# Late-mode forms in 128 rows, and fillers that move TensorE's instruction fetches, in a fused linear-attention and spectral-mix kernel

## The chip, the cores and the metric

The kernel runs on one core of a Trainium2 chip. The time is the device time of that core in microseconds (us), as the median of several executions. Before the change it was 421.37 us over 3 runs (421.35 to 421.74). The profile is one further execution of the same program; its span, from the first instruction to the last, was 419.6 us before. A stretch of the trace is given in us from the start of that span.

Besides the views of the profile, this document uses the packet records of the trace: start, duration, queue and size of every DMA packet. They carry no engine number; the *packets in flight* are counted over all engines together. A load of weights or a store ends with 16 small completion marks, one from each DMA engine, and the distance from the first mark to the last is called its *spread* here.

## The reference, cut to what matters

```python
def _attn_ref(q, k, v):                       # (8, 8, 576, 64) each
    q_p, k_p = (phi(q), phi(k))
    kv = np.einsum('bhsd,bhse->bhde', k_p, v)
    ...
    return (num / den).astype(np.float32)

def _moe_ref(x, w_r, w_i, w_ch):              # w_r, w_i: (64, 512, 512), w_ch: (512, 512)
    X = np.fft.rfft(x, axis=1)
    Xr, Xi = (np.real(X[:, :n_modes]), np.imag(X[:, :n_modes]))
    Yr = np.einsum('bmd,mde->bme', Xr, w_r) - np.einsum('bmd,mde->bme', Xi, w_i)
    Yi = np.einsum('bmd,mde->bme', Xr, w_i) + np.einsum('bmd,mde->bme', Xi, w_r)
    Y[:, :n_modes] = Yr + 1j * Yi
    y = np.fft.irfft(Y, n=S, axis=1)
    u = x + y
    return (u + np.maximum(u @ w_ch, 0.0)).astype(np.float32)
```

The 64 modes have two 512x512 weight matrices each. These are the bulk of the bytes, and each is used only once.

## The kernel before: the parts concerned

The modes are worked off in pairs. For each pair the weights arrive in one of two rotating buffers, TensorE makes the product `P`, and the result is turned into columns (`picks`). After every fourth pair eight modes are evicted from PSUM. Modes from 32 on ("late") go to `YL`. Work of the attention part and of the end is put between, in slots, and *fillers* (`keep_warm`, products of the identity whose result nobody reads) end a pair.

```python
    def keep_warm(n: int):
        for _ in range(n):
            pin(nc.tensor.matmul(last_ps[0], id16, wch16[:, 0, :]))
    ...
    def mode_pair(p: int):
        w = w_get(p)
        ...
        for dc in range(NDW):
            product(P, xz[p % 2][:, dc].rearrange("p h n -> p (h n)"), 32, w, dc, NDW)
        ...
        work_slot(p, "mid")
        picks(2 * p, st, 2)
        if p % 4 == 3:
            ...
                g = (kk - NF) // NL + 1
                pin(nc.vector.tensor_copy(out=YL[:, :, :, g, :], in_=mode_rows(yt_ps)))
        work_slot(p, "end")
        keep_warm(FILL.get(p, 0))
    ...
    FILL = {**{p: 7 for p in range(18, 27)}, 27: 9, 28: 5, 29: 6, 30: 4}
```

In the last pairs each batch's late modes are brought into two forms, `z` (times `w_ch`) and `y` (transposed). `YL` holds the rows of a batch once, 64 of them, and both halves of the 128 output rows are made from them by a matmul each:

```python
    def form_z(b: int):
        z_ps = bank(f"z{b}")
        for ec in range(NDC):
            yt = YL[:, ec].rearrange("p k g b -> p (k g) b")[:, :, b]
            for h in range(2):
                pin(nc.tensor.matmul(z_ps[HALVES[h], :], yt, wch16[:, ec, :], ...))
        pin(nc.scalar.copy(out=YZ[b][:, 1, :], in_=z_ps))
```

## Time and profile before

| quantity | before | view |
|---|---|---|
| time, median of 3 | 421.37 us | timed runs |
| end of the weights' stage | 387.71 us | chain of work that ended last |
| last rows' copy issued, after which stores run | 390.30 us | timeline |
| last store's marks | 417.52 to 418.09 us | packet records |
| instruction fetches of TensorE, the last of them | 24, at 396.4 us | queue table, packet records |

First the page: one line of the engines' busy time, and two groups of instructions (busy us and mean ns of one; after the second bar the idle time before them and what ended it).

```profile
PE 288.7 (69%) x3115; PEld 155.9 (37%) x3115; DVE 228.6 (54%) x499; ACT 154.2 (37%) x253; POOL 58.1 (14%) x100
...
L431 PE MATMUL P<-w,xz 128*32 128x512 bf16 x496 | 48.3, 530 | 64.3 <-DMA w<-in_moe_w_i_dram 61.8
...
L418 PE MATMUL zl<-wch,id 128*128 128x512 f16 x93 | 23.0, 380 | 0.0
```

The products of the pairs (L431) wait 64.3 us in sum, 61.8 of it for weights: TensorE is not what bounds this stage. The fillers (L418) wait for nothing. The forms and the late eviction, in the view of the tile `YL` (ns: least, median, largest; then first and last start):

```profile
L710 PE MATMUL z<-wch,YL x64: 379/379/493, 352.6 to 380.3; 128*64 128x512 f16 x64
...
L480 DVE CAST YL<-yt x3: 681/691/692, 276.1 to 351.8; 128x512 f16<-128x512 f32 x3
```

There are 64 half-wide `z` matmuls and three large evictions. Last, a row of the table of windows from the stretch without fillers (columns: length, busy us of PE, PEld, DVE, ACT and POOL with counts, clock, DMA share, GB/s):

```profile
157.00:176.00 19.00, 7.20 (x88) 2.96 (x87) 6.00 (x18) 1.89 (x5) 1.77 (x5) 0.50 1.00 214
```

TensorE is busy 7.20 of 19 us, at half clock, with DMA full.

### The profile page before, as it was taken

How to read it: one execution, taken by the hardware profiler on the slowest of the kernel's cores; microseconds unless marked ns; L12 is line 12 of the kernel's file. 1: busy time of each engine (PE TensorE's matmuls, PEld its weight loads, DVE VectorE, ACT ScalarE, POOL GpSimd, SP SyncE). 2: the span in 40 equal slices, each digit the busy share in tenths (PEclk: the TensorE clock that was granted, in tenths of full speed). 3: DMA queues.
4: the chain of work that ended last, by engine and by line, in shares of the span. 5: the costliest groups of instructions: out<-in, count | busy, mean ns of one | idle time of the engine just before them, and what ended most of it. 6: DMA issues, size and time to landing. Idle time of an engine off the chain costs nothing.

```text
span 419.6 us, 7400 instructions
## 1 busy us (share of the span) xinstructions
PE 288.7 (69%) x3115; PEld 155.9 (37%) x3115; DVE 228.6 (54%) x499; ACT 154.2 (37%) x253; POOL 58.1 (14%) x100
## 2 busy tenths in 40 slices
PE   0359799899517553444343685998798878899993
PEld 0247677787301221222121232433343324354421
DVE  4587979994404462464645353454455433512794
ACT  4677888954101011000000233344253422230782
POOL 4222224210001111111111111111111111130000
PEclk9999958989655555555555589799899989999997
DMA  8999999999999999999999999999999999998698
GB/s 219 211 212 216 210 221 206 229 206 222 222 217 212 213 223 211 216 222 209 220 220 205 225 220 205 225 215 209 224 217 208 225 216 209 223 205 162 230 395 328
DMA packets 17073, 93.17 MB, mean 222 GB/s; under 512 B 2112, under 2 KB 3024, under 8 KB 12880
## 3 DMA queue, kind: packets, MB, share of 16 engines
q0 software_dynamic: 12496, 81.48, 93.3%
q1 hardware_dynamic: 4544, 11.22, 7.2%
q8 instruction: 24, 0.39, 0.3%
q14 instruction: 9, 0.07, 0.0%
HBM read 163.93 MB, written 9.44 MB: 413 GB/s over the span
## 4 chain that ended last, share of the span: by engine, by line
DMA 65%; PE 19%; DVE 5%; issue 3%; ACT 3%; POOL 2%; DVEq 0%; ACTq 0%; POOLq 0%
DMA w<-in_moe_w_i_dram 52%; DMA pick_sb<-row_pick 8%; PE P L431 7%; DMA k<-in_k_dram 5%; PE acc L747 3%; PE acc L787 2%; PE kvp L256 2%; ACT ke L207 2%; POOL w L116 2%; PE eps L688 1%; DVE x L292 1%; DVE ke L220 1%; POOL w L128 1%; DVE k L214 1%; PE zl L418 0%
## 5 line engine op out<-in xcount | busy, mean ns | idle before, releaser
L431 PE MATMUL P<-w,xz 128*32 128x512 bf16 x496 | 48.3, 530 | 64.3 <-DMA w<-in_moe_w_i_dram 61.8
L448 ACT CAST ys<-P 128x512 f16<-128x512 f32 x15 | 8.8, 585 | 131.6 <-PE P L431 131.6
L116 POOL DMA_DIRECT2D w<-in_moe_w_r_dram x31 | 17.8, 575 | 244.2 <-PE P L431 240.7
L431 PEld LDWEIGHTS <-xz 128*32 128x32 bf16 x496 | 13.2, 115 | 85.5 <-DMA w<-in_moe_w_i_dram 56.9
L446 DVE CAST ys<-P 128x512 f16<-128x512 f32 x17 | 11.8, 691 | 53.5 <-PE P L431 53.5
L688 PE MATMUL eps<-wch,xTw 128*128 128x512 f16 x144 | 40.6, 409 | 0.0
L162 PEld LDWEIGHTS <-qT 64*128 64x128 f16 (+1 forms) x640 | 22.8, 124 | 31.7 <-issue 17.2
L671 ACT CAST x16w<-x_main 128x512 f16<-128x512 f32 x32 | 19.8, 618 | 37.7 <-DVE x_main L669 37.7
L669 DVE TENSOR_TENSOR x_main<-ya,x_main 128x512 f32<-128x512 f32 x32 | 22.0, 691 | 18.7 <-PE ya L665 18.5
L256 PE MATMUL kvp<-vpad,ke 32*128 32x130 f16 x576 | 23.3, 255 | 9.1 <-ACT qT L243 6.4
L441 DVE COPY xz<-xt_c 64x256 bf16<-64x256 bf16 x62 | 22.9, 370 | 12.1 <-PE P L431 11.3
L696 ACT CAST E<-eps 128x512 f16<-128x512 f32 (+1 forms) x40 | 21.2, 539 | 19.5 <-PE eps L688 19.5
L256 PEld LDWEIGHTS <-ke 32*128 32x128 f16 x576 | 21.4, 113 | 10.8 <-issue 8.9
L162 PE MATMUL nw<-kv,qT 64*128 64x65 f16 (+1 forms) x320 | 18.9, 240 | 9.5 <-DVE x_tail L632 4.5
L418 PE MATMUL zl<-wch,id 128*128 128x512 f16 x93 | 23.0, 380 | 0.0
L292 DVE TENSOR_TENSOR x<-num,rd 128x512 f16<-128x512 f32 x32 | 22.1, 692 | 1.1
L236 PE MATMUL qTp<-id,qe 128*128 128x128 f16 x144 | 14.3, 278 | 11.7 <-DVE qe L220 9.5
L632 DVE TENSOR_TENSOR x_main<-nw,rd 128x256 f32<-128x256 f32 x32 | 11.2, 417 | 17.3 <-PE nw L162 17.3
L207 ACT ACTIVATE qe<-q 128x1152 f16<-128x1152 f16 (+1 forms) x16 | 17.9, 1157 | 7.5 <-DMA q<-in_q_dram 7.4
L454 PE MATMUL yt<-pick_sb,ys 128*128 128x32 f16 (+1 forms) x128 | 8.8, 186 | 16.9 <-DMA pick_sb<-row_pick 10.7
L680 DVE COPY xTw<-xTp 128x512 f16<-128x512 f16 x36 | 15.0, 416 | 10.0 <-PE xTp L678 9.9
L243 ACT COPY qT<-qTp 128x1152 f16<-128x1152 f16 x16 | 19.6, 1291 | 0.5 <-PE qTp L236 0.2
(118 smaller groups left out, 494.6 us busy)
## 6 DMA issues: line engine op xcount, KB each, us to landing
w<-in_moe_w_r_dram POOLq DMA_DIRECT2D x31, 1024.0 KB, 12.5
w<-in_moe_w_i_dram POOLq DMA_DIRECT2D x31, 1024.0 KB, 16.7
out_dram<-x_main SPq DMA_DIRECT2D x12, 512.0 KB, 3.8
k<-in_k_dram POOLq DMA_DIRECT2D x8, 576.0 KB, 13.1
v<-in_v_dram POOLq DMA_DIRECT2D x8, 576.0 KB, 14.4
q<-in_q_dram POOLq DMA_DIRECT2D x7, 576.0 KB, 12.8
out_dram<-x_main SPq DMA_DIRECT2D x8, 256.0 KB, 3.8
q<-in_q_dram SPq DMA_DIRECT2D x2, 576.0 KB, 4.5
```

The source lines that it names most:

```text
L116: nc.gpsimd.dma_start(out=w_in[p][half::2], in_=two.rearrange("g (r dc) e -> (g r) dc e", dc=NDW))
L162: mm = nc.tensor.matmul(num[hpo][orow, c0 : c0 + 65], qT[rows, hpp, h2, cols], kv_sb[rows, hpp, h2, :])
L207: pin(nc.scalar.activation(out=ev[:, c], in_=heads(nm, b, c), func=AF.Exp))
L256: nc.tensor.matmul(kv_ps[:, h2, 0:130], phi["k", b][r0 : r0 + 32, j // NJ, j % NJ].rearrange("p o d -> p (o d)"), vp[r0 : r0 + 32, :, j, 0 ...
L292: nc.vector.tensor_tensor(out=dst.rearrange("p (o c d) -> p o c d", o=2, c=4), in0=nv[:, :, :, 0:64], in1=rden.unsqueeze(3).broadcast_to([ ...
L418: pin(nc.tensor.matmul(last_ps[0], id16, wch16[:, 0, :]))
L431: nc.tensor.matmul(P[c : c + n, :], x, w[:, dc, :], start=(dc < NDC), stop=(dc >= n_dc - NDC), tile_position=(0, c), skip_group_check=True,)
L441: pin(nc.vector.tensor_copy(out=xz[p % 2][HALVES[h], :, h, :], in_=src))
L669: pin(nc.vector.tensor_tensor(out=x, in0=acc, in1=x, op=ALU.add))
L671: pin(nc.scalar.copy(out=x16w[t], in_=x))
L688: nc.tensor.matmul(e_ps, xT[:, c, :], wch16[:, c, :], start=(c == 0), stop=(c == NDC - 1))
L696: pin(nc.scalar.copy(out=dst, in_=e_ps[:, cols]))
```

## The change

The rows of a batch are kept twice in `YL`, now split over two tiles, so that one full-width matmul makes all 128 rows of a form: 64 matmuls fewer. The forms move out of pair 30, and pairs 28 to 30 get more fillers in their place. Pairs 5 to 15 (modes 10 to 31) get seven fillers each. By the words of the change these are there to shift TensorE's instruction fetches.

```diff
-    FILL = {**{p: 7 for p in range(18, 27)}, 27: 9, 28: 5, 29: 6, 30: 4}
+    FILL = {**{p: 7 for p in range(5, 16)}, **{p: 7 for p in range(18, 27)}, 27: 7, 28: 10, 29: 12, 30: 10}
...
+    def late_modes(g: int, ps):
+        ...
+        for h, yl in enumerate(YL):
+            rows = mode_rows(ps)[:, h * (NDC // 2) : h * (NDC // 2) + NDC // 2]
+            for d in range(2):
+                pin(nc.vector.tensor_copy(out=yl[:, :, d, :, g, :], in_=rows))
...
         for ec in range(NDC):
-            yt = YL[:, ec].rearrange("p k g b -> p (k g) b")[:, :, b]
-            for h in range(2):
-                pin(
-                    nc.tensor.matmul(
-                        z_ps[HALVES[h], :], yt, wch16[:, ec, :],
-                        start=(ec == 0), stop=(ec == NDC - 1), skip_group_check=True,
-                    )
-                )
+            pin(
+                nc.tensor.matmul(
+                    z_ps, late_rows(ec, b), wch16[:, ec, :], start=(ec == 0), stop=(ec == NDC - 1)
+                )
+            )
...   (form_y in the same way)
     share(
         n_form,
-        [((first_form, "end"), 6)]
+        [((first_form, "end"), 8)]
         + [((p, h), 4) for p in range(first_form + 1, LAST - 1) for h in ("mid", "end")]
-        + [((LAST - 1, "mid"), 2), ((LAST - 1, "end"), 1)],
+        + [((LAST - 1, "mid"), 0), ((LAST - 1, "end"), 0)],
     )
```

The second tile takes the place of the attention part's `kv` tiles, which are merged into one tile for that.

More of the change, by code (lines that the diff above doesn't have):

```diff
@@ L100 @@
     q_tile = lambda name: xpool.tile([128, QW], F16, tag="qTE", bufs=B, name=name)
-    kv_all = [xpool.tile([128, 2, 2, 65], F16, tag="kv", bufs=B, name=f"kv{b}") for b in range(B)]
+    kv_sb = xpool.tile([128, B, 2, 2, 65], F16, tag="kv", bufs=1, name="kv_sb")
+    kv_all = [kv_sb[:, b] for b in range(B)]
     rd_all = [xpool.tile([128, 5, 2, 4], F32, tag="rd", bufs=B, name=f"rd{b}") for b in range(B)]
@@ L479, in mode_pair @@
                 g = (kk - NF) // NL + 1
-                pin(nc.vector.tensor_copy(out=YL[:, :, :, g, :], in_=mode_rows(yt_ps)))
+                late_modes(g, yt_ps)
         work_slot(p, "end")
@@ L541, with late_rows @@
     YE_T = ystage.tile([128, NDC, NF, 2 * B], F16, name="YE_T")
-    YL = ystage.tile([128, NDC, 2 * NL, NF // NL, B], F16, name="YL")
+    YL = [ystage.tile([128, NDC // 2, 2, 2 * NL, NF // NL, B], F16, name="YL0")]
     Y8 = ystage.tile([128, NDC, NL, 2 * B], F16, name="Y8")
-    nc.vector.memset(YL[:, :, :, 0, :], 0.0)
+    def late_modes(g: int, ps):
+        if len(YL) == 1:
+            YL.append(
+                xpool.tile([128, NDC // 2, 2, 2 * NL, NF // NL, B], F16, tag="kv", bufs=1, name="YL1")
+            )
+            for yl in YL:
+                pin(nc.vector.memset(yl[:, :, :, :, 0, :], 0.0))
+        for h, yl in enumerate(YL):
+            rows = mode_rows(ps)[:, h * (NDC // 2) : h * (NDC // 2) + NDC // 2]
+            for d in range(2):
+                pin(nc.vector.tensor_copy(out=yl[:, :, d, :, g, :], in_=rows))
+    def late_rows(ec: int, b: int):
+        yl = YL[ec // (NDC // 2)][:, ec % (NDC // 2)]
+        return yl.rearrange("p d k g b -> p (d k g) b")[:, :, b]
     def mode_rows(ps):
@@ L720, in form_y @@
         for ec in range(NDC):
-            yt = YL[:, ec].rearrange("p k g b -> p (k g) b")[:, :, b]
-            for h in range(2):
-                pin(nc.tensor.transpose(y_ps[HALVES[h], ec, :], yt, id16))
+            pin(nc.tensor.transpose(y_ps[:, ec, :], late_rows(ec, b), id16))
         pin(nc.vector.tensor_copy(out=YZ[b][:, 0, :], in_=y_ps.rearrange("p c r -> p (c r)")))
```

## The prediction

> **What bounds the kernel now.** I read the page first: the slices, the DMA queues, the chain that ended last.
>
> ```profile
> PEclk9999958989655555555555589799899989999997
> DMA  8999999999999999999999999999999999998698
> ...
> q0 software_dynamic: 12496, 81.48, 93.3%
> q1 hardware_dynamic: 4544, 11.22, 7.2%
> q8 instruction: 24, 0.39, 0.3%
> ...
> DMA 65%; PE 19%; DVE 5%; issue 3%; ACT 3%; POOL 2%; DVEq 0%; ACTq 0%; POOLq 0%
> ```
>
> The DMA row is at 9 from the second slice to the 36th, and DMA is 65% of the chain. The 24 packets of the queue called instruction (0.39 MB, so 16 KB each) are the fetches that the change names. Then the chain in order of time, at a late pair of modes and at the end:
>
> ```profile
> 349.86 1.01 PE P L431 x16
> 350.87 0.29 issue
> 351.16 0.54 POOL w L116
> 351.69 16.66 DMA w<-in_moe_w_i_dram
> ...
> 386.75 0.36 PE y_last L512 x8
> ...
> 410.55 1.23 DVE x_main L821
> 411.82 1.23 DVE x_tail L821
> 413.05 1.13 DVEq L1007
> ```
>
> A load of weights is issued when a product has freed its buffer, and takes 16.66 us to land because the load before it is still running. So I asked whether a late product ever lets the DMA run dry. The trace's packet records (start, duration, size of every packet) say no: summed over packets, 16 engines are at work in every nanosecond from 20 to 382 us. Then the stage after the weights, in the table of windows:
>
> ```profile
> 384.00:388.00 4.00, 3.60 (x45) 1.67 (x41) 1.32 (x2) 0.00 (x0) 0.00 (x0) 1.00 0.51 91
> 388.00:391.00 3.00, 2.67 (x23) 1.71 (x23) 1.26 (x4) 1.38 (x4) 0.43 (x1) 1.00 0.00 0
> ...
> 406.00:410.00 4.00, 4.00 (x25) 1.09 (x24) 4.00 (x4) 3.58 (x7) 0.00 (x0) 1.00 1.02 407
> 410.00:414.00 4.00, 2.45 (x16) 0.67 (x12) 3.92 (x4) 2.20 (x5) 0.00 (x0) 1.00 1.02 407
> ```
>
> The columns are PE, PEld, DVE, ACT and POOL busy, the clock, the DMA share and GB/s. The reader should see three stages: saturated weights until 384, a hole at 388 to 391 in which nothing is moved, and stores that saturate DMA again (1.02, 407 GB/s), with PE and DVE just as full.
>
> The packet records add what no view shows: the last packets of one load of weights do not end together. The 16 completion marks of a load spread over 0.44 us at 20 us, 1.5 after the fetch at 25.9, 2.6 after the one at 94.6, and 3.72 after the one at 255.2, then 3.84 to the end. Each fetch (0.9 to 1.0 us) holds up one engine; eight fetches go round eight engines, and the next round starts over. In the end the fastest engines finish the weights at 383.9 and the slowest at 387.7. **The slowest engine, with its three fetches, ends the stage.** The 24th fetch, at 396.4, is in the store stage: the spread of a store's completions goes from 0.65 us to 1.41 with it, and is still 0.57 at the last store, at 418.1.
>
> **What the skill says.** "Runtime: NRT & Kernel Launch", section Instruction fetch mechanics: instructions come in 16 KiB blocks of 256, fetched by the sequencer's own DMA queue ahead of need. The trace agrees: 24 packets of 16384 bytes, 253 recorded PE instructions apart on average. "DMA: Bandwidth & Descriptors", section Queues, rings and completion order: a DMA engine takes turns between the rings that have work; so a fetch delays the weights of its engine only, as the spreads show. "TensorE: Matmul & The Clock Gate", Part 3: matmuls in different column groups run at the same time. The trace agrees: eight half-wide z matmuls take 1.14 us from first start to last end, four full ones of another group 1.03. Part 1 there says that the clock is at half or full after idle or busy windows of some 3.4 us: the records of the granted clock hold only 0.5 and 1.0, and it is 0.5 from 110.8 to 243.9 us.
>
> **The change, part by part.** (1) *128-row forms.* Per batch, 8 of 16 matmuls go, with their weight loads: 64 matmuls, 128 instructions. By the 1.14 and 1.03 us above that is 0.1 us per z, and 0.58 to about 0.40 for a y: 8 x 0.3 = 2.3 us of PE, beside the weights. On the path: 0. (2) *Rows kept twice.* Each of three 512-element evictions (0.69 us) becomes four of 256. A 256-element DVE instruction from PSUM takes 0.42 us in the rows of line 632, so 4 x 0.42 - 0.69 = 1.0 us more, three times, plus two memsets of some 0.3 instead of one. DVE is about half busy there. At pair 27 the forms wait for it: 1 us of PE. On the path: 0, as long as (3) holds. (3) *Fillers.* 11 pairs x 7 = 77, and -2, +5, +6, +6 at pairs 27 to 30: 92 matmuls. In the cold stretch seven of them take 7 x 0.43 = 3.0 us, and PE works some 4 of each pair's 9.7 us there, so 7 of 9.7. Products start 0.33 us after their weights and the next load is issued 4.4 us before the fastest engine would run dry; at pair 15, where PE is the busiest, 3.2. At pair 5 a slack of 2.2 left no idle time. So even 3 us of delay at pair 16 could leave only the fastest engines idle, and those wait 2.7 us for the slowest at the end of a load anyway. On the path: 0. If the fillers lift the clock to 1.0 for part of 140 to 240 us, products take 1.05 us instead of 1.9, also at no gain. (4) *The sum of instructions*: -128 + 2 x 92 = +56 on PE. A block boundary behind all the edits comes 56 instructions earlier in the program. The 24th fetch was seen with 6050 matmuls and loads started. Fifty-six before that is 5994, which PE starts at about 389.3 us, just where it waits for the last rows. It would then fall in the hole of 388 to 391, where no transfer can be held up. The fetch count stays 24, so still three fetches on the slowest engine, and the weights end at 387.7 +- 0.2. (5) *The store stage* loses 16 KB (0.04 us at 407 GB/s) and one engine's delay, 0.57 us at the last store. But two other engines end 0.4 to 0.5 late, after small fetches of other engines at 403.5 and 407.3. So the sure gain is 0.1 us, the most 0.6. I choose 0.3: 421.37 - 0.3 = 421.05, rounded.
>
> **Rivals.** *The fetch only moves within the store stage, or later*, since PE's sequencer runs ahead of PE by an amount I read only roughly (it varied by over 100 instructions between fetches). For it: that wobble. Against: PE stalls at 388.3 and 390, when the sequencer gets furthest ahead. Later by some us it would cost 0.2 to 0.5: 421.4 to 421.8. *PE becomes the bound in the cold pairs*: fillers delay products past the slack and the loads come late. Against: 3 us of fillers against 3.2 to 4.4 of slack, and the spread beside. If the slowest engine did starve, 1 to 2 us: 422.5 to 423.5. *The forms are what limits the end*: then 2.3 us of PE and lighter last pairs would show, up to 419. Against: PE waits for weights after them (1.28 us idle before the product at 378.1), and DMA never stops. *A chance drop of the clock*: a window at 0.5 falls in the store stage, +1 us; the larger fillers of pairs 28 to 30 speak against it.
>
> **Range and chances.** The likely paths lie between 420.7 and 421.5; the three runs before span 0.4; a missed wait adds above, an unseen gain of a few tenths below. 8 in 10: 420.3 to 421.7. A gain of 2% is 8.4 us, and no part of the sum has it: faster 0.01, same 0.97, slower 0.02.
>
> **What would show it.** Right: still 24 instruction packets, the 24th between 388 and 391.5; spread of the last store under 0.5 us; the last load's spread again 3.7 to 3.9 and its end at 387.7; 16 engines at work to 382; some 3143 matmuls; DVE busy up by 3 to 4 us. Wrong: 23 or 25 fetches, engines idle between 130 and 380, the weights' end moved by over 0.3 us, or a gain with the 24th fetch still among the stores.

## The result

The changed kernel took 421.22 us (median of 6 runs, 421.14 to 421.42), and the kernel before 421.38 (6 runs of the same rounds, 421.28 to 421.74). The ratio is 0.9996, with a 95% interval of 0.9983 to 1.0009: the same. Ratios here are the mean time of one kernel's fast runs over that of the other's of the same rounds, so not quite the ratio of the medians quoted. All runs named in this document gave the reference's result.

The page of the changed kernel, with the lines that answer to those of before:

```profile
PE 317.2 (76%) x3143; PEld 164.4 (39%) x3143; DVE 231.3 (55%) x509; ACT 154.2 (37%) x253; POOL 57.4 (14%) x100
...
PEclk9999999579855658665655599899899997899998
DMA  8999999999999999999999999999999999998698
...
q0 software_dynamic: 12496, 81.48, 93.4%
q1 hardware_dynamic: 4544, 11.22, 7.2%
q8 instruction: 24, 0.39, 0.3%
...
DMA 64%; PE 23%; DVE 4%; POOL 3%; ACT 3%; issue 2%; DVEq 0%; ACTq 0%; POOLq 0%
...
L432 PE MATMUL P<-w,xz 128*32 128x512 bf16 x496 | 42.6, 475 | 37.6 <-DMA w<-in_moe_w_i_dram 35.4
L419 PE MATMUL zl<-wch,id 128*128 128x512 f16 x185 | 58.2, 466 | 0.0
```

TensorE is busy 28.5 us longer, which is less than the 35.2 us that 92 more fillers add (58.2 - 23.0). The products became shorter because the clock is now partly up between 120 and 240 us, and they wait 37.6 us instead of 64.3. Nothing of this reaches the DMA row, which is digit for digit that of before. A busier and faster TensorE has only waited less for the same weights. The windows say the same:

```profile
157.00:176.00 19.00, 10.26 (x108) 4.28 (x107) 6.79 (x20) 1.89 (x5) 2.17 (x4) 0.77 1.01 215
384.00:388.00 4.00, 3.57 (x44) 1.63 (x43) 1.32 (x2) 0.00 (x0) 0.00 (x0) 1.00 0.53 94
388.00:391.00 3.00, 2.67 (x22) 1.72 (x23) 1.34 (x4) 1.47 (x4) 0.51 (x1) 1.00 0.02 5
406.00:410.00 4.00, 4.00 (x26) 1.11 (x26) 3.99 (x4) 3.56 (x7) 0.00 (x0) 1.00 1.02 406
```

In 157 to 176 PE is busy 10.26 us instead of 7.20 at a clock of 0.77 instead of 0.50, and DMA moves 215 GB/s instead of 214. The hole at 388 to 391 has a DMA share of 0.02 instead of 0.00 and 5 GB/s: **one instruction fetch of 16 KB now falls into it**. By the packet records it is the 24th, at 389.52 us. The chain in order of time:

```profile
369.52 1.01 PE P L432 x16
370.52 0.29 issue
370.81 2.16 POOL w L129 x4
372.98 13.65 DMA w<-in_moe_w_i_dram
386.67 0.36 PE y_last L513 x8
...
410.46 1.22 DVE x_main L834
411.75 1.23 DVE x_tail L834
412.97 1.13 DVEq L1020
```

The chain goes through the load of the last pair's weights and ends with the same three entries, each some 0.1 us earlier. The `YL` tile:

```profile
L726 PE MATMUL z<-wch,YL x32: 379/379/644, 351.8 to 374.6; 128*128 128x512 f16 x32
...
L557 DVE CAST YL<-yt x12: 362/415/425, 275.7 to 351.9; 128x256 f16<-128x256 f32 x12
```

Half the `z` matmuls at the same median of 379 ns; twelve evictions of 415 ns in place of three of 691, which is 12 x 0.415 - 3 x 0.691 = 2.9 us of DVE. The last form starts 5.7 us earlier (374.6 instead of 380.3).

Where the span moved is best told by four points of time, which I use for every kernel here. The *hole*, the stretch in which DMA moves almost nothing, is measured from the weights' end to the issue of the copy of the last rows; *stores* runs from there to the last mark of the last store.

| kernel (PE matmuls) | weights end | hole | stores | of it the last spread | last fetch | span |
|---|---|---|---|---|---|---|
| before (3115) | 387.71 | 2.59 | 27.79 | 0.57 | 24th, 396.4 | 419.57 |
| after (3143) | 387.62 | 2.59 | 27.71 | 0.43 | 24th, 389.5 | 419.41 |

0.09 us come from the weights' end and 0.08 from the stores, of the 0.16 of the span. Each row is a single trace, and the weights' end alone differs by 0.16 us between runs in which no engine is seen dry (experiment 9), so these tenths are not shown to be the change's.

### The profile page after: what moved, and what is told of

Its sections match the earlier page's. It is cut to its first block, busy times and chain, and to the rows that moved or that the text cites. A ratio compares the mean times of both kernels' runs of the same rounds, so it can differ in the third digit from the quotient of the medians.

```text
span 419.4 us, 7466 instructions
## 1 busy us (share of the span) xinstructions
PE 317.2 (76%) x3143; PEld 164.4 (39%) x3143; DVE 231.3 (55%) x509; ACT 154.2 (37%) x253; POOL 57.4 (14%) x100
## 4 chain that ended last, share of the span: by engine, by line
DMA 64%; PE 23%; DVE 4%; POOL 3%; ACT 3%; issue 2%; DVEq 0%; ACTq 0%; POOLq 0%
DMA w<-in_moe_w_i_dram 53%; DMA pick_sb<-row_pick 8%; PE P L432 6%; DMA k<-in_k_dram 3%; PE acc L760 3%; PE kvp L257 3%; PE acc L800 2%; POOL w L117 2%; PE z L726 1%; DVE x L293 1%; ACT ke L208 1%; PE xf L355 1%; PE zl L419 1%; PE qTp L237 1%; PE num L163 1%
## 5 line engine op out<-in xcount | busy, mean ns | idle before, releaser
L432 PE MATMUL P<-w,xz 128*32 128x512 bf16 x496 | 42.6, 475 | 37.6 <-DMA w<-in_moe_w_i_dram 35.4
L419 PE MATMUL zl<-wch,id 128*128 128x512 f16 x185 | 58.2, 466 | 0.0
L706 PE MATMUL eps<-wch,xTw 128*128 128x512 f16 x144 | 39.3, 399 | 0.0
L257 PE MATMUL kvp<-vpad,ke 32*128 32x130 f16 x576 | 24.3, 263 | 8.9 <-ACT qT L244 6.1
L442 DVE COPY xz<-xt_c 64x256 bf16<-64x256 bf16 x62 | 23.0, 371 | 10.9 <-PE P L432 10.0
L419 PEld LDWEIGHTS <-id 128*128 128x128 f16 x185 | 18.9, 112 | 25.6 <-issue 14.3
L257 PEld LDWEIGHTS <-ke 32*128 32x128 f16 x576 | 22.3, 116 | 10.6 <-issue 8.6
L163 PE MATMUL nw<-kv_sb,qT 64*128 64x65 f16 (+1 forms) x320 | 18.2, 231 | 9.8 <-DVE x_tail L650 4.7
## 6 DMA issues: line engine op xcount, KB each, us to landing
w<-in_moe_w_r_dram POOLq DMA_DIRECT2D x31, 1024.0 KB, 13.2
```

Of the source, the lines that this page charges most:

```text
L163: mm = nc.tensor.matmul(num[hpo][orow, c0 : c0 + 65], qT[rows, hpp, h2, cols], kv_sb[rows, hpp, h2, :])
L257: nc.tensor.matmul(kv_ps[:, h2, 0:130], phi["k", b][r0 : r0 + 32, j // NJ, j % NJ].rearrange("p o d -> p (o d)"), vp[r0 : r0 + 32, :, j, 0 ...
L432: nc.tensor.matmul(P[c : c + n, :], x, w[:, dc, :], start=(dc < NDC), stop=(dc >= n_dc - NDC), tile_position=(0, c), skip_group_check=True,)
L442: pin(nc.vector.tensor_copy(out=xz[p % 2][HALVES[h], :, h, :], in_=src))
L706: nc.tensor.matmul(e_ps, xT[:, c, :], wch16[:, c, :], start=(c == 0), stop=(c == NDC - 1))
```

## The experiments

My theory was the prediction's: the weights' stage is paced by the DMA engine that was held up by the most fetches, TensorE's work beside it is free, and the only gain lies in where the 24th fetch falls. The rivals were that the shorter forms pay by themselves, that the fillers are needed for the clock, and that late products would starve the DMA. Times are medians with the range and the number of runs. The ratios rest on means, and in some a few slow draws of the kernel before (up to 424.15 us) pull them towards 1; the medians and the traces say more. The four-point table of all runs follows the last experiment.

**1. The same edits with the old number of instructions (same_count).** The early fillers are cut from 77 to 49, so that PE has the 3115 matmuls of before.

```diff
-    FILL = {**{p: 7 for p in range(5, 16)}, ...
+    FILL = {**{p: 5 if p < 10 else 4 for p in range(5, 16)}, ...
```

> The changed kernel with 49 instead of 77 fillers in pairs 5 to 15, so PE has exactly the instruction count of the kernel before (3115 matmuls); forms, doubled rows and late fillers stay. Mine (only the place of the last fetch matters): the 24th fetch goes back to 395 to 398 us, among the stores; spread of the last store 0.5 to 0.7 us instead of 0.43; time that of the kernel before, 421.38 +- 0.15. Rival (the 128-row forms bring the gain): fetch back, but time stays at 421.2 or less.

The 24th fetch went back to 397.3 us, among the stores, and the last store's spread to 0.60 us. The count does place the fetch. The time was 421.48 us (421.03 to 422.10, 6) against 421.46 for before (421.32 to 423.28, 11), ratio 0.9996. The spans of the two traces, 419.78 and 419.41, differ by a third of a microsecond; that cannot be told apart by these times.

**2. Only the fetch moved (moved_alone).** The kernel before with 28 early fillers, so 3143 matmuls with the old forms.

```diff
-    FILL = {**{p: 7 for p in range(18, 27)}, 27: 9, ...
+    FILL = {**{p: 3 if p < 11 else 2 for p in range(5, 16)}, **{p: 7 for p in range(18, 27)}, 27: 9, ...
```

> The kernel before with 28 fillers added in pairs 5 to 15 (56 PE instructions, as many as the change adds net), nothing else of the change. Mine: 24th fetch at 388 to 391 us, in the hole between weights and stores, one engine fewer late at the last store, spread 0.4 to 0.5 us; time 421.2 +- 0.15, that of the changed kernel. Rival (forms bring the gain): 421.38.

The fetch came at 391.6 us, in the hole, which in this run was open until 392.2. But the time was 421.85 us (421.13 to 423.36, 6), scattered and not better. The profiled run is the slowest of the six (423.36). In it the clock was at half from 359.2 to 362.7 and from 366.1 to 372.9 us, the last products were late, and TensorE reached the last rows with work left over: 56 matmuls in 388 to 392 us where the kernel before has 26. The hole grew to 4.13 us. The expectation failed: to move the fetch alone is worth nothing measurable, and less than the spread of this kernel's times, of which the half clock may be the cause (only this draw was traced). The last spread, too, stayed at 0.66 us where 0.4 to 0.5 was expected. The packet records have a cause that the experiment had left out: queue q14 makes instruction fetches of 8 KB, and two of them fall among the stores, at 403.5 and 407.3 us before the change, at 405.4 and 409.2 here, but at 393.9 and 407.2 in the changed kernel. In every run with the new forms the first of the two comes 3.5 to 3.7 us after the copy of the last rows is issued, in every run with the old forms 13.2 to 13.3 us after it. So the change moves two fetches, and this run moved one.

**3. The forms without any new filler (forms_alone).** The changed kernel with the `FILL` line of before (3051 matmuls).

> The 128-row forms, the doubled rows and their new places, with the fillers of the kernel before: PE has 128 instructions fewer than before. Mine: the forms are beside the weights, so the end of the weights stays at 387.6 +- 0.3 us and 16 engines stay at work from 20 to 382; the block boundary that made the 24th fetch lies behind the end of the program, so 23 fetches, or a 24th at the very end; time 421.2 +- 0.2. Rival 1 (forms save on the path): 420 or less. Rival 2 (fillers at the end were needed for the clock): a granted clock of 0.5 after 388 and 422 or more.

This is the slowest of the first four: 423.50 us (422.53 to 423.63, 6), ratio 1.0039 (1.0024 to 1.0055). I had expected that the 24th fetch might go away; it came, at 411.5 us. Against the changed kernel's trace the span is 2.46 us longer: 0.28 at the weights' end, 0.75 in the hole, 1.40 in the stores. The hole shows in the windows, the changed kernel first, then this one:

```profile
388.00:393.00 5.00, 4.65 (x30) 2.57 (x31) 3.20 (x7) 3.45 (x8) 0.57 (x1) 1.00 0.31 88
```

```profile
388.00:393.00 5.00, 4.88 (x29) 2.50 (x28) 1.90 (x4) 1.91 (x5) 0.57 (x1) 0.66 0.10 21
```

The same work takes longer at a mean clock of 0.66; the clock's records have 0.5 from 389.2 to 392.6 us. Here TensorE *is* the path, so a window at half clock costs. Of the 1.40 us in the stores, 0.95 goes with the fetch: at 411.5 us little time is left to absorb it, and the last spread is 1.38 us instead of 0.43. The other 0.45 is the same half clock, which lasts 1.4 us into the stores: the first five products there take 1.88 us instead of 1.42.

**4. A fourth round of fetches (fourth_round).** The changed kernel with 250 tiny matmuls (16 columns) more, 25 at the end of each of the pairs 5 to 14. They are nearly free for TensorE but bring two more fetches.

```diff
+    TINY = {p: 25 for p in range(5, 15)}
+    def keep_tiny(n: int):
+        for _ in range(n):
+            pin(nc.tensor.matmul(last_ps[0][:, 0:16], id16, wch16[:, 0, 0:16]))
...
         keep_warm(FILL.get(p, 0))
+        keep_tiny(TINY.get(p, 0))
```

> The changed kernel with 25 matmuls of 16 columns added in each of pairs 5 to 14: 250 matmuls, 500 PE instructions, nearly two blocks more, about 2.7 us of PE per pair where it has over 4 to spare. Mine (the engine with the most fetches ends the weights): 26 fetches, two of them a fourth on their engine, at about 340 to 380 us; the spread of the last loads 4.4 to 4.8 us instead of 3.4; weights end 0.9 to 1.0 us later, at 388.5; time 422.1 +- 0.2. Rival (fetches are too small to matter, 16 KB in 93 MB): 421.2 +- 0.1, the spread stays at 3.4.

The queue table has the two fetches more:

```profile
q8 instruction: 26, 0.43, 0.4%
```

The weights ended at 388.74 us, 1.12 later than in the changed kernel, while hole and stores stayed within 0.05. The time was 422.50 us (422.40 to 422.75, 6), ratio 1.0020 (1.0005 to 1.0036), 0.4 above the 422.1 that I had named. The spread of the last loads is 4.5 us instead of 3.3 to 3.4, as expected (4.4 to 4.8). Before the weights' end 25 fetches have come (the 25th at 376.5 us, the 26th only at 393.1) instead of 23. If they go round eight engines, the 24th ends the third round and the 25th begins a fourth: one packet of 16 KB on an engine that had three already. The size of the loss agrees with the duration of one fetch, 0.89 to 1.12 us in the trace of the changed kernel.

The packet records bear out the turn of eight in three ways. The durations of nearly all fetches beside the loads repeat with a period of eight (in the trace of before 935, 975, 974, 961, 893, 893, 948, 945 ns, then 935 again for the 9th and the 17th). The spread of the loads takes a lasting step of some 1 us with the 1st, the 9th, the 17th and, only here, the 25th fetch (0.4 to 1.5, 1.5 to 2.5, 2.6 to 3.6, 3.5 to 4.5 us), and none so large with the fetches between. And of the 16 marks of the last load eight come by 386.3 us, seven at 387.4 to 387.7 and a single one at 388.7, as it would be with eight engines without fetches, seven with three and one with four.

**5. The changed kernel again (after_again).** An unchanged copy. It was run at another time.

> The changed kernel once more, for the spread of its times beside more of the kernel before. In the first four experiments 3 of 11 times of the kernel before were 422.4 to 423.3 and the rest 421.3 to 421.5. Theory 1 (the larger fillers of pairs 28 to 30 keep the granted clock at 1.0 from about 360 us to the end whatever the phase of its windows): all six of this within 421.0 to 421.6, while some of the kernel before are over 422. Theory 2 (slow draws come to both alike): one or two of six over 422.

421.53 us (421.20 to 421.83, 5) against 421.44 for before (421.24 to 421.77, 9), ratio 1.0003 (0.9989 to 1.0016). The trace repeats the 24th fetch (389.7 us) and the last spread of 0.43 us. So the mechanism repeats and the gain in time does not: its sign is not settled. The question that I had put, whether slow draws come to the kernel before alone, stays open: none of its nine times is above 421.77.

**6. Late fillers only (no_early_fill).** The changed kernel without its 77 early fillers (3066 matmuls).

```diff
-    FILL = {**{p: 7 for p in range(5, 16)}, **{p: 7 for p in range(18, 27)}, 27: 7, ...
+    FILL = {**{p: 7 for p in range(18, 27)}, 27: 7, ...
```

> The changed kernel without the 77 fillers of pairs 5 to 15; forms and late fillers stay. It parts the two losses of forms_alone (423.5): a granted clock of 0.5 after 389, and a 24th fetch at 411 us among the last stores. Theory 1: the clock stays at 1.0 after 360, so the hole is as short as in the changed kernel (first store landed at 393.1 +- 0.3); the 24th fetch is at 395 to 412, depending on how far the sequencer is ahead, and the spread at the last store is 0.6 to 1.3 us; time 421.5 to 422.2. Rival (the early fillers are what keeps the clock up): 423.5 as forms_alone.

422.19 us (422.07 to 422.95, 5), ratio 1.0021 (1.0009 to 1.0034). The weights end within 0.16 us of the changed kernel's, the hole is 2.61 us with the clock at full, and all the rest of the 1.00 us in the span lies in the stores, 0.83, with a last spread of 1.34 us: the 24th fetch fell at 406.3. The late fillers are all in which this run differs from experiment 3, and the hole of 3.34 us with its half clock is gone, in one trace of each; the times, 422.07 to 422.95 against 422.53 to 423.63, go the same way. This divides the loss of experiment 3: **the late fillers hold the clock up in the hole, and the early fillers keep the fetch away from the last stores.** Neither gains against the kernel before; both repair what the shorter forms would cost.

**7 and 8. Products made late (late_product, very_late_product).** All of pair 10's share is raised, to 45 and to 64 fillers, so that the product of pair 11 comes late and its buffer is freed late.

```diff
-    FILL = {**{p: 7 for p in range(5, 16)}, ...
+    FILL = {**{p: 45 if p == 10 else 7 for p in range(5, 16)}, ...   (64 in the second)
```

> The changed kernel with 45 fillers instead of 7 at pair 10, so that the product of pair 11 comes some 5 us later than its weights (0.4 in the changed kernel). Mine (fast engines wait for the slowest anyway): fast engines run dry for 1 to 2 us near 199, the spread of the loads after it falls from 2.3 to about 1.2 us, the slowest engine never stops and the weights end at 387.6 +- 0.3; time that of the changed kernel within 0.3. Rival (any dry engine costs time): 1 to 2 us longer.

> The same with 64 fillers at pair 10: the product of pair 11 comes some 9 us late. Mine: all 16 engines run dry near 199, the slowest for about 3 us, and the time is longer by just that, 2 to 4 us; spread of the loads after it under 0.8 us. Rival (the stream has slack elsewhere to catch up): under 1 us longer.

The product came 7.8 us late, where I had aimed at 5 (some of the fillers ran at half clock), and 10.9 us late in the second. I sum, from the packet records, by how many the packets in flight fall short of 16: 34.3 and 83.7 engine-us from 20 to 382 us, where the kernel before and the changed one have none. (Small packets raise the sum to 17 and up to 20 for about a fifth of the time between 150 and 382 us, so a sum of 16 nearly shows, but does not prove, that no engine stood still.) The windows show it, the changed kernel first, then late_product:

```profile
196.00:204.00 8.00, 5.47 (x55) 2.18 (x54) 5.08 (x16) 0.00 (x0) 0.45 (x1) 0.64 0.99 212
```

```profile
196.00:204.00 8.00, 6.29 (x65) 2.88 (x63) 2.63 (x7) 0.59 (x1) 1.09 (x2) 1.00 0.74 136
```

The DMA share falls from 0.99 to 0.74. The weights ended 2.29 and 5.44 us later, close to the idle time per engine (34.3 / 16 = 2.1 and 83.7 / 16 = 5.2). The times were 424.15 us (423.59 to 424.76, 4), ratio 1.0064, and 429.02 us (428.28 to 430.64, 4), ratio 1.0185, which at 2% is unclear. In both a 25th fetch came, at 412.3 and 410.9 us, and added 1.0 us to the stores; the hole of the second is 0.62 us longer as well. Both expectations failed, the first because the product came later than aimed at; the second cost about twice what I had expected. Late products are a real danger, then, and it begins only past the slack.

**9. A product late within the spread (late_within).** The same 77 early fillers, 34 of them at pair 10.

```diff
-    FILL = {**{p: 7 for p in range(5, 16)}, ...
+    FILL = {**{p: 34 if p == 10 else 5 if p < 8 else 4 for p in range(5, 16)}, ...
```

> The changed kernel with the same 77 early fillers differently shared: 34 at pair 10 and 4 or 5 at the others, so the product of pair 11 is late by some 5 to 6 us (7.8 in late_product, where all 16 engines ran dry and time rose by 2.7) and the place of the fetches behind stays. Mine (fast engines have time to wait that the slowest has not): the fast engines run dry for 1 to 2 us near 200, the slowest does not; the spread of the loads falls by that much, to under 1.8 us, while the weights still end at 387.5 to 387.9; time 421.4 +- 0.3. Rival (what any engine loses is lost): weights end 1 to 2 us later.

The product was 4.99 us late. Some engines ran dry from 199.45 to 200.13 us, 2.2 engine-us in sum, and the spread of the load fell from 2.56 to 1.64 us. So the fastest engines lost 0.9 us of their lead. The weights' end moved by 0.20 us against the changed kernel, 0.11 against the one before, and about that much differs between runs in which no engine is seen dry (387.62 to 387.78 among after, before, warm_alone and no_early_fill is a range of 0.16). The time was 421.60 us (421.10 to 422.09, 6), ratio 0.9997 (0.9979 to 1.0015). Idle time of engines that would have waited for the slowest anyway was free, as far as this can show. The last spread of 0.55 us, with the 24th fetch at the same 389.7 us as in after_again (0.43), has another cause: up to 407 us it is 0.38, and with an 8 KB fetch of q14 at 407.4 us, which took 0.77 us here, it jumps to 0.88 and has fallen to 0.55 at the end.

**10. The late fillers with the old forms (warm_alone).** The kernel before with the changed kernel's fillers in pairs 27 to 30 (3130 matmuls).

```diff
-    FILL = {**{p: 7 for p in range(18, 27)}, 27: 9, 28: 5, 29: 6, 30: 4}
+    FILL = {**{p: 7 for p in range(18, 27)}, 27: 7, 28: 10, 29: 12, 30: 10}
```

> The kernel before with only the late fillers of the change (7, 10, 12, 10 at pairs 27 to 30); its 64-row forms and their places stay. 15 matmuls, 30 PE instructions more. Theory 1 (the forms had to become shorter and leave pair 30 for these fillers to fit): the products of pairs 29 and 30 come over 2.5 us late, fast engines run dry near 370, and the hole between weights and first row copy is over 2.6 us; time 422 to 424, or one run in two. Rival (the fillers alone do it, the forms are of no use): 421.2 to 421.5.

423.16 us (422.43 to 427.79, 6), ratio 1.0051 (1.0014 to 1.0088). I had expected dry engines near 370 us. There were none, and the products were late by 1.3 and 1.9 us only. The loss lies in the hole, 3.56 us with the clock at full all the way. In this window TensorE still has 56 matmuls to do, where the changed kernel's row above has 30:

```profile
388.00:393.00 5.00, 4.64 (x56) 2.87 (x53) 2.17 (x5) 2.43 (x6) 0.56 (x1) 1.00 0.09 18
```

The last product had been pushed back by work of pair 30. So the late fillers have room only beside the new forms. Whether their being shorter or their having left pair 30 gives it was not tested apart. The two parts of the change need each other: each alone lost.

**11 and 12. An attempt to beat both (balanced, balanced_five).** If the slowest engine ends the stage, the last weights should go to the engines with the fewest fetches. The second half-load of pair 29 (64 rows) is cut into transfers of 48, 8 and 8 rows, and of 48, 5, 5 and 6 rows, to give the shorter ones to fewer engines.

```diff
+        rows_in = two.rearrange("g (r dc) e -> (g r) dc e", dc=NDW)
+        cuts = (0, 48, 56, 64) if (p, half) == (29, 1) else (0, 64)      # (0, 48, 53, 58, 64)
+        for lo, hi in zip(cuts, cuts[1:]):
+            pin(nc.gpsimd.dma_start(
+                out=w_in[p][half + 2 * lo : half + 2 * hi - 1 : 2], in_=rows_in[lo:hi]))
```

> The changed kernel with one load (imaginary half of pair 29) cut into 48, 8 and 8 rows, so that the 16 rows taken out go to 8 engines only, if an 8-row transfer always uses the same 8. Theory (the spread of engines at the end of the weights is worth up to half its 3.4 to 3.8 us): if these are the engines without instruction fetches, the spread of the last loads falls by about 2.4 us and the weights end about 1.2 us earlier, time 420.1 to 420.5; if they are the engines with the fetches, the spread grows by 2.4 us and the time by 1.2, 422.4 to 422.8; if the choice goes round, little changes.

> As balanced, but the load is cut into 48, 5, 5 and 6 rows. In balanced 13 engines ended the weights at 385.2 to 386.5 us (five at 384.4 and nine at 387.3 to 387.6 in the changed kernel) and three at 388.4: so most of the spread went, and three late engines seem to have been among the eight that took the extra rows. If the five engines that end first are the first five to be filled: all engines end at 386.9 or before, 0.7 us earlier, time 420.6 +- 0.3. If others are: the last engine ends at 389 to 390 and the time is 423 or more. That is a guess at even odds; the trace has no engine numbers.

In the first, 13 of 16 engines finished the weights by 386.5 us (in the changed kernel seven finish by 384.8, two by 386.6 and seven at 387.3 to 387.6), but one finished at 387.4 and two at 388.4. The counts of five, nine and three engines in the expectation for balanced_five do not come out of these marks. The work was shifted, though not only away from the slow engines. The times were 422.27 us (421.99 to 422.47, 6), ratio 1.0014, and 422.53 us (422.28 to 422.71, 6), ratio 1.0013, so neither beats the kernels (by the medians of their calls they are 0.9 and 1.0 us slower than before); the weights ended at 388.43 and 389.08 us. Which engines take a small transfer cannot be read from packet records without engine numbers, so it stays open whether another cut would win.

**All four points.** Each row is one profiled run; *short* is the engine-us by which packets in flight fall short of 16 from 20 to 382 us.

| kernel (PE matmuls) | weights end | hole | stores | last spread | last fetch | short |
|---|---|---|---|---|---|---|
| forms_alone (3051) | 387.90 | 3.34 | 29.11 | 1.38 | 24th, 411.5 | 2.7 |
| no_early_fill (3066) | 387.78 | 2.61 | 28.54 | 1.34 | 24th, 406.3 | 0 |
| before (3115) | 387.71 | 2.59 | 27.79 | 0.57 | 24th, 396.4 | 0 |
| same_count (3115) | 387.86 | 2.59 | 27.85 | 0.60 | 24th, 397.3 | 2.0 |
| warm_alone (3130) | 387.69 | 3.56 | 27.92 | 0.65 | 24th, 395.6 | 0 |
| moved_alone (3143) | 388.09 | 4.13 | 27.91 | 0.66 | 24th, 391.6 | 6.5 |
| after (3143) | 387.62 | 2.59 | 27.71 | 0.43 | 24th, 389.5 | 0 |
| after_again (3143) | 387.70 | 2.61 | 27.66 | 0.43 | 24th, 389.7 | 0.8 |
| late_within (3143) | 387.82 | 2.61 | 27.76 | 0.55 | 24th, 389.7 | 2.2 |
| balanced (3143) | 388.43 | 2.67 | 27.65 | 0.42 | 24th, 390.4 | 0.6 |
| balanced_five (3143) | 389.08 | 2.66 | 27.71 | 0.47 | 24th, 391.2 | 0.1 |
| late_product (3181) | 389.91 | 2.65 | 28.75 | 1.50 | 25th, 412.3 | 34.3 |
| very_late_product (3200) | 393.06 | 3.21 | 28.74 | 1.27 | 25th, 410.9 | 83.7 |
| fourth_round (3393) | 388.74 | 2.63 | 27.76 | 0.34 | 26th, 393.1 | 0.2 |

From the top to 3143 matmuls the 24th fetch comes earlier with each step of the count, from 411.5 to about 390 us. The column of the stores falls with it, from 29.1 to 27.7. What falls is the last spread: the stores less the last spread are 27.2 to 27.3 us in every row but forms_alone (27.7, the half clock), very_late_product (27.5) and fourth_round (27.4). Nearly all of that drop is already had at 396 us; the last step, from 396 to 390, is worth about 0.1 us and lies inside what runs of one count differ by (spreads of 0.42 to 0.66 at 3143). The changed kernel therefore sits at the flat end of a curve on which the kernel before already was.

## Why the prediction was right or wrong

The outcome, the same within 2%, was foreseen, and 421.22 lies in the range. Point by point:

- **Forms, off the path: right.** 64 matmuls went, and the last form starts 5.7 us earlier without any gain; forms_alone shows no gain, but a loss. The rival that the forms limit the end is refuted. (One reading beside it was too wide: in the stores the lines shown have DVE full to 414 us, but PE to 410 only, with 2.45 of 4 us after that.)
- **Doubled rows: right.** Twelve evictions of 415 ns (0.42 said). DVE is busy 231.3 instead of 228.6 us, so 2.7 more, a little under the 3 to 4 said.
- **Fillers, off the path: right, with room.** The packets in flight never fall under 16 from 20 to 382 us in the changed kernel, and the weights end at 387.62 us (387.7 +- 0.2 said). The experiments 7 to 9 put the edge: 5.0 us late was free, 7.8 us cost 2.3 us at the weights' end.
- **Three fetches on the slowest engine: right.** A 25th fetch before the weights' end, the first of a fourth round, went with an end 1.12 us later, and one engine alone was late by it. The spread of the last loads was 3.31 to 3.43 us, though, not 3.7 to 3.9. In the repeat it was 3.71 up to 368 us and 2.83 at the end, after some engines had run dry for 0.8 engine-us, and the weights still ended at 387.70. So that sign was badly chosen: the spread depends on the fastest engine, the end on the slowest.
- **The fetch moves into the hole: right.** It came at 389.52 us (388 to 391.5 said, 389.3 worked out), and the last spread was 0.43 us (under 0.5 said). Both repeated in after_again. The prediction knew the 8 KB fetches at 403.5 and 407.3 but took them to stay; the first moved to 393.9, so the smaller last spread is not the 24th fetch's alone. same_count, where the 8 KB fetches lie as in the changed kernel (394.0 and 407.5) and the 24th at 397.3, has 0.60, which favours the 24th; late_within has 0.55 with the 24th in the hole.
- **The size of the gain: too large.** The failing term is in step (5), where I chose 0.3 us between a sure 0.1 and a most of 0.6. The traces have 0.08 us in the stores and 0.14 in the last spread. A fetch at 396 us has some 20 us of stores behind it: in the trace of before, the spread of a store's marks rises from 0.65 to 1.41 us with it and has fallen to 0.57 at the last store. So the sure gain was nearly all there was. In the repeat even the sign was lost. The tenths cannot be claimed from the times.
- **What I under-weighted: the clock and the larger fillers.** I dismissed a chance drop of the clock in one sentence and priced the late fillers only as off the path. The runs show that they are part of the bargain: the forms with the late fillers alone cost 0.75 us by the medians against the kernel before, and with neither set 2.0 us. I also feared for the fetch mainly that it might come later by some us at 0.2 to 0.5 us; at 406 to 412 us it costs about 1.

The kernel before had 7 runs of 48 above 422.3 us (up to 424.15), the changed one none of 11 (at most 421.83). A steadier time would be a sensible aim of such fillers. But in the two calls that hold those 11 runs the kernel before has none above 422.3 in 15 either, so they compare nothing. In the calls in which it has 7 of 33, the runs nearest to the changed kernel are same_count and late_within, with none of 12 (at most 422.10); at a share of 7 in 33 that would come by chance in 6% of cases ((26/33)^12). So this is not shown. What set those slow draws was not traced; moved_alone's profiled run, with two windows at half clock, is only a candidate.

## What to carry to other kernels

When the DMA engines are full, ask which engine ends last and what only that engine has to carry: one 16 KB fetch on the wrong engine or near the last store cost about 1 us here, and thousands of idle or busy TensorE cycles beside the loads cost nothing, as long as no product came over 5 us late. Before crediting a shortening of work beside the bound, test it alone: here it lost 2 us, because with fewer instructions the last fetch came late and the clock was at half in the one place where TensorE is the path. And a shift of a fetch can be seen in the trace where the tenths that it may be worth cannot be told from what differs between runs.

## What the Trainium skill lacked or had wrong

- "Runtime: NRT & Kernel Launch", section Instruction fetch mechanics, calls the cost of crossing a 16 KiB block one tail bump, "mostly hidden". In a kernel bound by DMA its transfer is not: each fetch took 0.89 to 1.12 us, going from 23 to 25 fetches before the end of the weights moved that end by 1.12 us, and a fetch at 406 or 411 us among the last stores raised the last spread from 0.43 to 1.34 and 1.38 us.
- The same section does not say how fetches are shared out over the DMA engines. Here the spreads of the loads (1.5, 2.6 and 3.7 us from the 1st, the 9th and the 17th fetch on), the durations that repeat with a period of eight, and the single late engine of fourth_round fit eight engines in turn; no record here has an engine number, so this is inferred.
- "DMA: Bandwidth & Descriptors", section Why a DMA increments its semaphore by 16 and not by 1, says that a transfer from GpSimd over fewer than 16 engines takes consecutive ones from a round-robin cursor. It does not say how to know where that cursor stands, and no record here has it, so the rule could be neither used nor checked: a load cut to 48, 8 and 8 rows left two engines at 388.4 us where thirteen had finished by 386.5.
